# Attention, experts and a tanh-shrink layer in one program: a redrawn opening plan (first scores, small softmax steps, first loads)

## The chip, the core and the metric

The kernel is one program on one core of a Trainium2 chip. The metric is the device time of one execution in microseconds (us), the lower the better; a kernel's time is the median of three executions. Inputs and outputs lie in the core's HBM.

## What is computed

Three layers follow each other, all in float32. The first is local attention: 2 batches, 8 heads, 576 positions, head size 64. Four heads see the last 32 positions ("plain"), four see every fourth of the last 128 ("dilated").

```python
scores = np.where(masks, scale * q @ k.T, -1e9)
attn = np.exp(scores - scores.max(-1)); attn /= attn.sum(-1) + 1e-9
x = (attn @ v)                      # then heads side by side: 1152 x 512
p = domain_probs / (domain_probs.sum(-1) + 1e-9)
x = sum(p[:, e] * (np.maximum(x @ w1[e], 0) @ w2[e]) for e in range(4))   # 512 -> 1024 -> 512
h = x @ w_in;  g = h - np.tanh(h);  out = g @ w_out                       # 512 -> 2048 -> 512
```

## The kernel before, in words

Tokens are handled in two sets, 512 and 640. Each hidden layer is cut into slices of 512 features; a slice needs two loads of `w1` (512 KB each, tile `raw`), two of `w2`, and each weight is split into a high part (a copy) and a low part (a subtraction), tiles `w`. A product is then three matmuls: high by high, high by low, low by high. The activations `x` and hidden values `h` are split in the same way. From the third slice on, the first product is done by a seven-product scheme.

The program isn't written in the order in which it runs. Every operation is first recorded with a duration (`Engine.cost`), its tiles and what it depends on; then the class `Order` lays the operations out in time, engine by engine, several times, and for the first part of the program tries 1,200 random shifts of the due times. What it settles on is emitted, and each engine then runs its own list strictly in that order. So one cost changed in the table can move instructions on every engine. Because one helper records all operations, nearly all rows of the trace carry one line (L331; L729 for loads); tiles tell them apart.

The part that matters here is `first_attention`, for the 512 tokens of the first set. The work is cut into two halves by position, each of plain and dilated heads, so eight softmax "keys", numbered 0 to 7: keys 0 to 3 belong to the first half (0, 1 plain; 2, 3 dilated), 4 to 7 to the second. For a half:

- `open` writes the mask into a PSUM bank with a matmul (tile `p`, 128x384); `scores` adds q by k onto it (64x96 matmuls, `bank<-x,x`);
- `softmax` takes the maximum on VectorE, and then goes one of two ways, by `STYLE`. Style 1: subtract the maximum (VectorE), one exponential over 128x384 (ScalarE), one sum (VectorE). Style 0: four exponentials of 128x96 on ScalarE, each with its own bias and sum (`accum_out`), and two steps on 128x4 that scale the maximum and add 1e-9;
- a multiplication on GpSimd by one over the sum, then `transposes` on TensorE (`bank<-ident,att`), a copy by ScalarE (`w<-bank` 96x512), and `values` (`bank<-w,h` 64x64, where `h` holds v);
- the result is copied to a high part (ScalarE), a low part (VectorE) and a whole.

After four `values` of the first half the first expert's product can begin (`bank<-x,w` 128x256): this document calls its first row the start of the stream. Matmuls of a zero tile (`warm`, tile `zero`) may be put in where TensorE would wait; eleven stand at the start (`WARM`), and more are offered at places in the list, where the planner leaves out those that don't fit.

Loads are all issued by SyncE, in the planner's order. A load that follows eight others waits for the landing of the one eight places before it.

Of the kernel before, what the change touches and what calls it, by code (L numbers as in the profile page):

```python
# [16 lines left out]
ACTF = mybir.ActivationFunctionType  # L17
# [202 lines left out]
class Program:  # L220
# [7 lines left out]
    def __init__(self):  # L228
        self.ops = []
        self.open = None  # L230
        self.fill = False
        self.seek = self.until = 0
        self.hold = None

    def op(self, engine, us, emit, outs=(), ins=(), port=False, data=0.0):
        if self.open is not None:
            assert engine == "tensor"
            self.open[0] += us
            self.open[1].append(emit)
            self.open[2].extend(outs)  # L240
            self.open[3].extend(ins)
            return
        o = Op()
        o.n, o.engine, o.us, o.emit, o.port, o.data = len(self.ops), engine, us, emit, port, data
        o.before, o.after, o.tiles = set(), [], []
        o.fill, o.gone = self.fill, False
        if self.hold is not None and engine not in ("tensor", "sync"):
            o.before.add(self.hold)
        o.tail = self.TAIL[engine]
        regions = {}  # L250
        for views, writes in ((ins, False), (outs, True)):
            for v in views:
                t, region = v if isinstance(v, tuple) else (v.tile, v.region())
                regions.setdefault((id(t), writes), (t, set()))[1].add(region)
        for (_, writes), (t, found) in regions.items():
            if t not in o.tiles:
                o.tiles.append(t)
            for host in t.hosts:
                if host not in o.tiles:
                    o.tiles.append(host)  # L260
            if o.fill == "idle" and t.ring.psum:
                if wrote_by := [n for n, wrote, _ in t.log if wrote]:
                    o.before.add(wrote_by[-1])
                continue
            found = _joined(found)
            for region in found:
                for other, wrote, region2 in t.log:
                    if (writes or wrote) and other != o.n and _meet(region, region2):
                        o.before.add(other)
            if writes:  # L270

                t.log = [
                    x for x in t.log
                    if not any(_covers(region, x[2]) for region in found) or x[0] == o.n
                ]
            t.log.extend((o.n, writes, region) for region in found)
        for t in o.tiles:
            t.touch.append(o.n)
        self.ops.append(o)
# [35 lines left out]
class Engine:  # L315
# [22 lines left out]
    def cost(self, method, kw, outs, ins):  # L338
        n = math.prod(outs[0].shape[1:])
        psum = any(v.tile.ring.psum for v in (*outs, *ins))  # L340
        if self.name == "tensor":
            rows = kw["lhsT"].shape[0] if method == "matmul" else 128
            if method != "matmul":
                return 0.155, False
            if kw["lhsT"].dtype == F32:
                return 0.055 if n == 96 else 0.071, False
            if kw["lhsT"].dtype == BF16:
                return n / 2400.0 + 0.047, False
            return n / 2400.0 + 0.0136, False
        if self.name == "scalar":  # L350
            if "accum_out" in kw:
                return 0.39, False
            each = 0.00183 if outs[0].real_strides()[-1] > 1 or n < 0 else 0.00083
            return (0.172 if any(v.tile.ring.psum for v in ins) else 0.205) + n * each, False
        if self.name == "vector":
            if method == "tensor_reduce":
                n = math.prod(ins[0].shape[1:])
                return 0.152 + n * 0.00105, False
            big = [v for v in ins if math.prod(v.shape[1:]) > 16]
            if psum:  # L360
                return 0.153 + n * 0.00104 + 0.05 * (len(ins) > 2), False
            if n <= 16:
                return 0.18, len(ins) > 1
            if method in ("tensor_tensor", "scalar_tensor_tensor"):
                return 0.15 + n * 0.00104, len(big) > 1
            return 0.16 + n * 0.00052, True
        if method == "tensor_tensor":
            spread = any(0 in v.real_strides() for v in ins)
            return 0.185 + n * (0.00168 if spread else 0.00217), True
        return 0.1 + n * 0.0025, True  # L370


NAMES = ("tensor", "vector", "scalar", "gpsimd", "sync")
# [289 lines left out]
def tile_local_attention_moe_tanhshrink(  # L663
# [56 lines left out]
    def bank(loose=False):  # L720
        return Tile(bank_r, [128, 512], F32, loose=loose).view()
# [11 lines left out]
    def load(view, src):  # L733
        dma(view, src, 4.0 * math.prod(view.shape))
# [170 lines left out]
    class Kind:  # L905
# [51 lines left out]
        def _v(self, t, j, part, b0, n):  # L957

            f = 4 * D
            o = self.parts[part][4][2] + b0 * f  # L960
            a = v[:, o:o + n * f]
            load(t[:, j * f:(j + n) * f], a)

        def load_v(self, i):
            t = self.v[i] = plain32(h_tile(self.g))
# [107 lines left out]

    far_ = {}

    STYLE, COLD, FAR = ((1, 0, 1, 0), (1, 0, 1, 0)), (0,), 6

    class Pair:

# [134 lines left out]
    class Piece(Pair):  # L1214
# [16 lines left out]

        def scores(self, half, c):
            m = masks[0, True]
            if half == 0:
                self.open((0, c), m if self.h.plain else m[:, :BK], not self.h.plain)
            elif c == 0:
                for a in range(2):
                    self.open((1, a), m[:, BK:2 * BK], True)
            with P.group():
                for part, j, qs, ks in self.h.scores(c):  # L1240
                    if j // 2 != half:
                        continue
                    for a in range(2):
                        n = 2 * (j % 2) + part // BQ
                        if half == 0:
                            to = self.sb[0, c][D * a:D * a + D, n * BK:(n + 1) * BK]
                        else:
                            n = 2 * c + j % 2
                            to = self.sb[1, a][part:part + BQ, n * BK:(n + 1) * BK]
                        pe.matmul(  # L1250
                            out=to, lhsT=qs[D * a:D * a + D, :], rhs=ks[D * a:D * a + D, :],
                            start=False, stop=True, skip_group_check=True,
                        )

        def cold(self, key):
            return key[0] in COLD
# [8 lines left out]
        def softmax(self, key):  # L1265
# [6 lines left out]
            if self.style(key):  # L1272
                d, _, _ = self.by_stack(t[:, 0], nm)
                dve.tensor_tensor(out=d, in0=s, in1=spread, op=ALU.add)
                p = self.with_eps(t)
                act.activation(out=p[:, :, :BK], in_=d, func=ACTF.Exp, scale=SCALE)
                dve.memset(ap=p[:, :, BK:], constant=1e-9)
                dve.tensor_reduce(out=r, in_=p, axis=AX.X, op=ALU.add)
                p = p[:, :, :BK]
            else:  # L1280
                act.activation(out=nm[:, :4], in_=nm[:, :4], func=ACTF.Copy, scale=SCALE)
                for j in range(4):
                    ks = slice(j * BK, (j + 1) * BK)
                    act.activation(
                        out=t[:, 1, ks], in_=self.sb[key][:, ks], func=ACTF.Exp,
                        bias=nm[:, j:j + 1], scale=SCALE, accum_out=sm[:, j:j + 1],
                    )
                p, _, _ = self.by_stack(t[:, 1], sm)
                act.activation(out=r, in_=r, func=ACTF.Identity, bias=eps[:, :1])
            dve.reciprocal(out=r, in_=r)  # L1290
            to, _, spread = self.by_stack(t[:, 0], sm)
            pool.tensor_tensor(out=to, in0=p, in1=spread, op=ALU.mult)
# [446 lines left out]
    def first_attention():  # L1739

        def score(half, i, *cs):
            for c in cs or (0, 1):
                both[i].scores(half, c)
# [16 lines left out]
            P.fill = False  # L1760

        idle = bank()
        warm(idle, WARM)
        score(0, 0, 0)
        soft(0)
        warm(idle, 6)
        score(0, 0, 1)
# [3 lines left out]
        warm(idle, 12)  # L1771
        score(0, 1, 1)
        soft(2, 3)
        turn(0)
        turn(1)
        use(0, 0, 0)
        score(1, 0)
        soft(4)
        turn(2)
        use(0, 0, 1)  # L1780
        soft(5)
        turn(3)
        use(0, 1, 0)
        score(1, 1)
        use(0, 1, 1)
        fill(*[("h", 0, 0, f) for f in range(NF)])
        soft(6)
# [42 lines left out]
    da.load_q_half(0)  # L1830
    da.load_k_half(0)
    pa.load_v(0)
    w_load(0, 0)
    da.load_v(0)
    w_load(0, 1)
    pa.load_piece(0, 1)
    pa.load_piece(1, 1)
# [17 lines left out]
    db.load_v_short()  # L1855
    first_exp = spare[1, True][:, :32]
    act.activation(out=first_exp, in_=zero, func=ACTF.Exp)
    P.op("gpsimd", 0.8, lambda: make_identity(nc, ident.real()), [ident], [], True)
    dve.tensor_copy(out=ident_bf, in_=ident)
    emit_consts()  # L1860
    emit_masks(0)
# [84 lines left out]
```

## Time and profile before

| what | value |
|---|---|
| median of three executions | 624.08 us (622.91 to 625.18) |
| profiled execution, its own time | 623.72 us |
| its span, first to last instruction | 621.7 us |
| TensorE busy | 616.5 us, 99% |
| TensorE weight loads busy | 542.8 us, 87% |
| VectorE, ScalarE, GpSimd busy | 379.5, 307.8, 316.1 us |
| mean granted clock of TensorE | 0.999 |

Times in rows are us from the start of the span. A row of the timeline holds a start, the time to the end of the last of its instructions, the engine, the operation with its tiles and its shape, and how many there were; idle time before it and what ended it stand in brackets. A float32 matmul shows as two records, so x16 there are 8 matmuls of the program. TensorE's busy time is nearly the whole span, but matmuls of the zero tile count in it as work.

### The profile page before, as it was taken

Reading aid. Unit: us, or ns where it says so; the run is one execution under the profiler, and the core shown is the slowest. Engines: PE = TensorE matmul, PEld = TensorE weight load, DVE = VectorE, ACT = ScalarE, POOL = GpSimd, SP = SyncE. Lnnn points to the kernel's source line nnn. Section 1 sums busy time; section 2 is a strip of 40 time slices with the busy share of each in tenths; the row PEclk is TensorE's granted clock in tenths of the full one; section 3 lists DMA queues with packets and bytes.
Section 4 is the critical chain, followed back from the end, with each engine's and each line's share of the span. In section 5 each row is a group of like instructions: output and inputs, shape, how many; then the busy total and the mean of one; then the engine's idle time right before and its main releaser. Section 6 shows DMA issues by size and latency. Waiting matters only on the chain.

```text
span 621.7 us, 10650 instructions
## 1 busy us (share of the span) xinstructions
PE 616.5 (99%) x4034; PEld 542.8 (87%) x4034; DVE 379.5 (61%) x718; ACT 307.8 (50%) x744; POOL 316.1 (51%) x284
## 2 busy tenths in 40 slices
PE   9999999999999999999999999999999999999997
PEld 5887798989889889889889889898898988998986
DVE  4856567877776777745424455446877667753652
ACT  6876675654434344424314355343775563551540
POOL 4659982845335435435425459863655563560220
PEclk9999999999999999999999999999999999999999
DMA  8984134164445456322102112330305324110012
GB/s 303 357 289 136 35 103 143 38 214 148 137 135 170 137 155 200 103 69 69 35 34 69 35 35 68 129 119 25 119 1 170 119 84 137 51 53 1 18 51 84
DMA packets 37266, 68.03 MB, mean 109 GB/s; under 512 B 4192, under 2 KB 11488, under 8 KB 37216
## 3 DMA queue, kind: packets, MB, share of 16 engines
q1 hardware_dynamic: 37216, 67.37, 33.2%
q8 instruction: 31, 0.51, 0.3%
q14 instruction: 19, 0.16, 0.1%
HBM read 56.61 MB, written 10.75 MB: 108 GB/s over the span
## 4 chain that ended last, share of the span: by engine, by line
PE 98%; DVE 1%; ACT 0%; issue 0%; DVEq 0%; ACTq 0%
PE bank L331 98%; DVE acc L331 0%; ACT att L331 0%; DVE bank L331 0%; DVE h L331 0%; DVE st L331 0%; DVEq L1942 0%; ACT p L331 0%; DVE att L331 0%; DVE zero L331 0%; DVE eps L331 0%; DVEq L331 0%; ACTq L331 0%
## 5 line engine op out<-in xcount | busy, mean ns | idle before, releaser
L331 PE MATMUL bank<-w,h 128*128 128x512 f32 (+1 forms) x1392 | 323.3, 384 | 0.3
L331 PE MATMUL bank<-x,w 128*128 128x256 f32 (+2 forms) x1992 | 287.3, 298 | 0.0
L331 PEld LDWEIGHTS bank<-x,w 128*128 128x128 f32 x1992 | 277.9, 188 | 9.9
L331 PEld LDWEIGHTS bank<-w,h 128*128 128x128 f32 (+1 forms) x1392 | 240.8, 185 | 50.9 <-DVE acc L331 0.9
L331 POOL TENSOR_TENSOR w<-raw,w 128x512 fp32r<-128x512 f32 x102 | 133.6, 1323 | 144.2 <-ACT w L331 141.2
L331 ACT ACTIVATE h<-bank 128x320 fp32r<-128x320 f32 (+3 forms) x168 | 68.5, 421 | 82.5 <-PE bank L331 65.4
L331 DVE SCALAR_TENSOR_TENSOR acc<-bank,pn,acc 128x512 f32<-128x512 f32 x59 | 44.3, 750 | 76.8 <-PE bank L331 76.6
L331 DVE TENSOR_TENSOR bank<-bank,p 128x320 f32<-128x320 f32 (+1 forms) x132 | 61.0, 466 | 35.2 <-PE bank L331 24.2
L331 ACT ACTIVATE w<-raw 128x512 fp32r<-128x512 f32 x108 | 67.2, 629 | 28.2 <-PE bank L331 21.7
L331 DVE SCALAR_TENSOR_TENSOR att<-att 128x512 int32<-128x512 int32 (+1 forms) x96 | 76.0, 802 | 1.6
L331 DVE SCALAR_TENSOR_TENSOR h<-bank,h 128x320 fp32r<-128x320 f32 (+2 forms) x124 | 55.9, 464 | 26.1 <-ACT h L331 25.1
L331 POOL TENSOR_TENSOR w<-sum,w 128x512 fp32r<-128x512 f32 x36 | 48.7, 1352 | 38.0 <-ACT w L331 37.9
L331 ACT ACTIVATE p<-bank 128x320 f32<-128x320 f32 (+1 forms) x88 | 35.8, 413 | 51.1 <-PE bank L331 50.7
L331 ACT ACTIVATE att<-bank 128x256 f32<-128x256 f32 (+3 forms) x78 | 32.2, 431 | 50.2 <-PE bank L331 42.9
L331 ACT ACTIVATE att<-att 128x512 f32<-128x512 f32 (+2 forms) x40 | 26.2, 655 | 27.7 <-DVE att L331 21.8
L331 DVE TENSOR_TENSOR acc<-bank,acc 128x512 f32<-128x512 f32 (+1 forms) x28 | 18.7, 672 | 33.1 <-PE bank L331 33.1
L331 POOL TENSOR_TENSOR h<-att,h 128x256 fp32r<-128x256 f32 (+1 forms) x28 | 21.8, 800 | 27.0 <-ACT h L331 26.2
L331 POOL TENSOR_TENSOR sum<-raw 128x512 f32<-128x512 f32 x12 | 15.6, 1300 | 34.8 <-DMA raw<-in 14.0
L331 ACT ACTIVATE w<-sum 128x512 fp32r<-128x512 f32 x36 | 22.6, 628 | 20.7 <-PE bank L331 18.9
L331 POOL TENSOR_TENSOR att<-att,st 128x480 f32<-128x480 f32 (+1 forms) x20 | 18.4, 927 | 10.5 <-DVE st L331 9.7
L331 DVE TENSOR_SCALAR att<-att 128x512 int32<-128x512 int32 x32 | 17.2, 538 | 8.9 <-DMA in<-att 7.0
L331 DVE TENSOR_TENSOR bank<-bank,att 128x256 f32<-128x256 f32 (+1 forms) x32 | 14.7, 462 | 9.4 <-ACT att L331 9.1
(72 smaller groups left out, 356.4 us busy)
## 6 DMA issues: line engine op xcount, KB each, us to landing
raw<-in_moe_w_dram SPq DMA_DIRECT2D x40, 512.0 KB, 4.0
att<-in_moe_w_in_dram SPq DMA_DIRECT2D x16, 512.0 KB, 4.6
att<-in_moe_w_out_dram SPq DMA_DIRECT2D x16, 512.0 KB, 4.9
in<-att SPq DMA_DIRECT2D x16, 256.0 KB, 4.0
out<-att SPq DMA_DIRECT2D x16, 256.0 KB, 3.9
raw<-in SPq DMA_DIRECT2D x8, 512.0 KB, 3.7
raw<-out SPq DMA_DIRECT2D x8, 512.0 KB, 3.6
h<-in_v_dram SPq DMA_DIRECT2D x7, 512.0 KB, 6.3
```

The source lines that it names most:

```text
L331: getattr(self.engine, method)(**real)
```

## The change

Seven edits:

- costs: zero-tile matmuls at the start are planned 1.65 times longer, the first half's scores 2 times; `accum_out` on PSUM 0.335 us instead of 0.39; VectorE's memset 0.07; GpSimd's memset and other steps shorter; the identity 0.52 instead of 0.8;
- `STYLE` of the first four keys goes from (1, 0, 1, 0) to (0, 0, 0, 0);
- the two 128x4 steps of style 0 go from ScalarE to VectorE;
- the mask openings of the first half are recorded by a function of their own, after the first scores;
- the second half's scores are recorded earlier, and as work that may fill a wait;
- the dilated v of the first half is recorded ahead of the first weights;
- every load of v takes 96 partitions instead of 128 (`[:BK]`).

```diff
+        if engine == "tensor":
+            us *= self.rate
...
-                return 0.39, False
+                return 0.335 if any(v.tile.ring.psum for v in ins) else 0.39, False
...
-            a = v[:, o:o + n * f]
-            load(t[:, j * f:(j + n) * f], a)
+            load(t[:BK, j * f:(j + n) * f], v[:BK, o:o + n * f])
...
-    STYLE, COLD, FAR = ((1, 0, 1, 0), (1, 0, 1, 0)), (0,), 6
+    STYLE, COLD, FAR = ((0, 0, 0, 0), (1, 0, 1, 0)), (0,), 6
...
-                act.activation(out=nm[:, :4], in_=nm[:, :4], func=ACTF.Copy, scale=SCALE)
+                dve.tensor_scalar(
+                    out=nm[:, :4], in0=nm[:, :4], scalar1=SCALE, scalar2=0.0, op0=ALU.mult, op1=ALU.add,
+                )
...
-                act.activation(out=r, in_=r, func=ACTF.Identity, bias=eps[:, :1])
+                dve.tensor_scalar(
+                    out=r, in0=r, scalar1=1e-9, scalar2=0.0, op0=ALU.add, op1=ALU.add,
+                )
...
+        P.rate = 1.65
         warm(idle, WARM)
+        P.rate = 1.0
+        both[0].begin(0)
         score(0, 0, 0)
+        both[0].begin(1)
+        both[1].begin(0)
+        both[1].begin(1)
         soft(0)
...
+        P.fill = True
+        score(1, 0)
+        score(1, 1)
+        P.fill = False
         turn(0)
         turn(1)
...
     pa.load_v(0)
+    da.load_v(0)
     w_load(0, 0)
-    da.load_v(0)
```

What the planner makes of it is seen in the lists of instructions. On TensorE, at the very start, the kernel before has eleven zero-tile matmuls and then, for each of the four groups of the first half, an opening and its scores (`p` is the mask, `bank` a PSUM bank, `x` q and k); these are the rows of the first three groups and what follows the fourth:

```order
L331 MATMUL bank_135<-x0_78,x0_72 64x96 x8
L331 MATMUL bank_158<-p_84 128x384
L331 MATMUL bank_158<-x0_82,x0_72 64x96 x8
L331 MATMUL bank_181<-p_84 128x384
L331 MATMUL bank_181<-x0_102,x0_96 64x96 x8
L331 MATMUL bank_204<-p_84 128x384
L331 MATMUL bank_204<-x0_102,x0_96 64x96 x8
L331 MATMUL bank_222<-zero_80 32x512
```

At the same place the changed kernel, after eight zero-tile matmuls, has:

```order
L334 MATMUL bank_130<-x0_80,x0_72 64x96 x8
L334 MATMUL bank_159<-p_82 128x384
L334 MATMUL bank_166<-p_82 128x384
L334 MATMUL bank_170<-p_82 128x384
L334 MATMUL bank_159<-x0_87,x0_72 64x96 x8
L334 MATMUL bank_166<-x0_107,x0_98 64x96 x8
L334 MATMUL bank_170<-x0_107,x0_98 64x96 x8
L334 MATMUL bank_230<-p_82 128x384
L334 MATMUL bank_236<-p_82 128x384
L334 MATMUL bank_243<-p_82 128x384
```

The three other openings now stand together behind the first scores, and behind the fourth group come the second half's openings and its plain scores in place of seven zero-tile matmuls. From there to the start of the stream the changed list holds one zero-tile matmul, where the kernel before has eleven.

On SyncE, behind the first six loads, which are the same, the kernel before issues (`h` from `in_v` is v, `raw` is a weight load, `x` is q or k):

```order
L729 DMA h0_109<-in_v_dram 128x1024
L729 DMA x0_72<-in_q_dram 128x256
L729 DMA x0_78<-in_k_dram 128x256
L729 DMA x0_72<-in_q_dram 128x256
L729 DMA x0_82<-in_k_dram 128x256
L729 DMA h0_147<-in_v_dram 128x1024
L729 DMA raw_156<-in_moe_w1_dram 128x2x512
L729 DMA raw_176<-in_moe_w1_dram 128x2x512
L729 DMA x0_183<-in_k_dram 128x768
L729 DMA x0_96<-in_q_dram 128x512
```

and the changed kernel:

```order
L734 DMA x0_72<-in_q_dram 128x256
L734 DMA x0_80<-in_k_dram 128x256
L734 DMA x0_72<-in_q_dram 128x256
L734 DMA x0_87<-in_k_dram 128x256
L734 DMA x0_147<-in_k_dram 128x768
L734 DMA x0_98<-in_q_dram 128x512
L734 DMA h0_161<-in_v_dram 96x1024
L734 DMA raw_172<-in_moe_w1_dram 128x2x512
L734 DMA raw_185<-in_moe_w1_dram 128x2x512
L734 DMA h0_190<-in_v_dram 96x1024
```

All q and k of the second half now go first, then the plain v, the two `w1` loads, and the dilated v last.

On VectorE, about when the weights land, the kernel before takes the first weight copy (`CAST w1`) between softmax steps (`st`, `att`) and low parts of x:

```order
L331 CAST w1_312<-raw_156 128x512
L331 TENSOR_REDUCE st_334<-bank_297 128x4
L331 RECIPROCAL st_291<-st_291 128x4
L331 TENSOR_TENSOR x0_352<-bank_281,x0_337 128x256
L331 TENSOR_REDUCE st_360<-bank_299 128x4
L331 TENSOR_TENSOR att_276<-bank_297,st_334 128x384
L331 CAST w1_378<-raw_176 128x512
```

and the changed kernel takes two copies in a row, from both loads:

```order
L334 TENSOR_REDUCE st_330<-bank_236 128x4
L334 TENSOR_REDUCE st_345<-bank_243 128x4
L334 CAST w1_356<-raw_172 128x512
L334 CAST w1_370<-raw_185 128x512
L334 TENSOR_SCALAR st_330<-st_330 128x4
L334 TENSOR_TENSOR att_382<-bank_243,st_345 128x384
L334 TENSOR_TENSOR x0_397<-bank_358,x0_354 128x256
```

The scaling of key 5's maximum (`st_330`) and the low parts of x now stand behind the copy from the second load.

About 30 us into the program the lists of all engines become the same again, in the same order to the end.

## Rows read from the trace of the kernel before

**Rows 1.** Waits of TensorE from 17 us to the end: total us, times, longest.

```profile
PE bank L331 <- DVE h L331: 0.3, 1, 0.3
```

**Rows 2.** Timeline of TensorE: start us, us, instruction, count.

```profile
1.01 4.88 PE L331 MATMUL bank<-zero 128*32 128x512 bf16 x11 [1.01 <-DVE zero L331]
5.81 0.39 PE L331 MATMUL bank<-p 128*128 128x384 bf16 x1
6.13 0.88 PE L331 MATMUL bank<-x,x 64*64 64x96 f32 x16
...
10.17 1.68 PE L331 MATMUL bank<-zero 128*32 128x512 bf16 x7
11.78 0.64 PE L331 MATMUL bank<-ident,att 128*96 128x128 f32 x4
12.36 0.39 PE L331 MATMUL bank<-zero 128*32 128x512 bf16 x1
...
13.24 0.69 PE L331 MATMUL bank<-w,h 96*64 96x64 f32 x16
13.86 0.50 PE L331 MATMUL bank<-p 128*128 128x384 bf16 x2
14.29 0.89 PE L331 MATMUL bank<-x,x 64*64 64x96 f32 x32
...
16.30 0.82 PE L331 MATMUL bank<-zero 128*32 128x512 bf16 x3
...
20.11 4.52 PE L331 MATMUL bank<-x,w 128*128 128x256 f32 x36
...
48.45 2.95 PE L331 MATMUL bank<-x,w 128*128 128x512 f32 x12
```

**Rows 3.** Timeline of VectorE, same columns.

```profile
7.06 0.56 DVE L331 TENSOR_REDUCE st<-bank 128x4 f32<-128x384 f32 x1 [3.46 <-PE bank L331]
...
10.27 0.18 DVE L331 RECIPROCAL st<-st 128x4 f32<-128x4 f32 x1
...
13.69 0.43 DVE L331 CAST w<-raw 128x512 fp32r<-128x512 f32 x1 [1.07 <-DMA raw<-in_moe_w_dram]
...
15.95 0.42 DVE L331 TENSOR_TENSOR x<-bank,x 128x256 fp32r<-128x256 f32 x1
```

**Rows 4.** Timeline of ScalarE, same columns.

```profile
8.96 0.34 ACT L331 ACTIVATE att<-bank,st 128x96 f32<-128x96 f32 x1
...
9.29 0.33 ACT L331 ACTIVATE att<-bank,st 128x96 f32<-128x96 f32 x1
...
10.39 0.30 ACT L331 ACTIVATE st<-st,eps 128x4 f32<-128x4 f32 x1
...
12.46 0.59 ACT L331 ACTIVATE w<-bank 96x512 f32<-96x512 f32 x1 [0.71 <-PE bank L331]
```

**Rows 5.** Timeline of GpSimd, same columns.

```profile
10.60 1.61 POOL L331 TENSOR_TENSOR att<-att,st 128x384 f32<-128x384 f32 x2 [5.57 <-DVE st L331]
...
14.20 1.27 POOL L331 TENSOR_TENSOR w<-raw,w 128x512 fp32r<-128x512 f32 x1 [0.99 <-DVE w L331]
...
42.68 1.30 POOL L331 TENSOR_TENSOR w<-raw,w 128x512 fp32r<-128x512 f32 x1 [2.09 <-ACT w L331]
```

**Rows 6.** Tile view, both `w1` loads: issue starts (first to last), then us to landing.

```profile
L729 SPq DMA_DIRECT2D raw<-in_moe_w_dram x2: 382/407/432, 6.5 to 7.3; - x2
...
DMA to landing us min/median/max: 7.1/7.4/7.7
```

**Rows 7.** The same view, both first v loads.

```profile
L729 SPq DMA_DIRECT2D h<-in_v_dram x2: 430/431/432, 3.5 to 6.1; - x2
...
DMA to landing us min/median/max: 5.8/6.0/6.3
```

**Rows 8.** The same view, dilated k of the first half.

```profile
L729 SPq DMA_DIRECT2D x<-in_k_dram x1: 442/442/442, 3.1 to 3.1; - x1
...
DMA to landing us min/median/max: 4.2/4.2/4.2
```

More of the change, by code (lines that the diff above doesn't have):

```diff
@@ L231, in __init__ @@
         self.fill = False
+        self.rate = 1.0
         self.seek = self.until = 0
@@ L358, in cost @@
                 return 0.152 + n * 0.00105, False
+            if method == "memset":
+                return 0.07, False
             big = [v for v in ins if math.prod(v.shape[1:]) > 16]
@@ L369, in cost @@
             return 0.185 + n * (0.00168 if spread else 0.00217), True
-        return 0.1 + n * 0.0025, True
+        return (0.15 + n * 0.00085 if method == "memset" else 0.15 + n * 0.0019), True
 NAMES = ("tensor", "vector", "scalar", "gpsimd", "sync")
@@ L1233, in scores @@
             m = masks[0, True]
-            if half == 0:
-                self.open((0, c), m if self.h.plain else m[:, :BK], not self.h.plain)
-            elif c == 0:
+            if half and c == 0:
                 for a in range(2):
                     self.open((1, a), m[:, BK:2 * BK], True)
+            P.rate = 1.0 if half else 2.0
             with P.group():
@@ L1253, in scores, with begin @@
                         )
+            P.rate = 1.0
+        def begin(self, c):
+            m = masks[0, True]
+            self.open((0, c), m if self.h.plain else m[:, :BK], not self.h.plain)
         def cold(self, key):
@@ L1762, in first_attention @@
         idle = bank()
+        P.rate = 1.65
         warm(idle, WARM)
+        P.rate = 1.0
+        both[0].begin(0)
         score(0, 0, 0)
+        both[0].begin(1)
+        both[1].begin(0)
+        both[1].begin(1)
         soft(0)
@@ L1776, in first_attention @@
         use(0, 0, 0)
-        score(1, 0)
         soft(4)
@@ L1783, in first_attention @@
         use(0, 1, 0)
-        score(1, 1)
         use(0, 1, 1)
@@ L1857, in tile_local_attention_moe_tanhshrink @@
     act.activation(out=first_exp, in_=zero, func=ACTF.Exp)
-    P.op("gpsimd", 0.8, lambda: make_identity(nc, ident.real()), [ident], [], True)
+    P.op("gpsimd", 0.52, lambda: make_identity(nc, ident.real()), [ident], [], True)
     dve.tensor_copy(out=ident_bf, in_=ident)
```

## The prediction

> **What bounds the kernel now.** I read TensorE's waits first: from 17 us to the end it waits 0.3 us in all [rows 1]. From there on the time is the sum of TensorE's own rows, and nothing that the other engines do there is on the path, unless it gets late. So the change can only act before, and what it gains must show as an earlier arrival at a row that both kernels have.
>
> Then I read TensorE's timeline ahead of that point [rows 2]. The reader should see there three kinds of rows: real ones, waits, and matmuls of the zero tile, which do no work but count as busy. There are 11 at the start (4.88 us, 0.44 each), 7 at 10.17, 1 at 12.36 and 3 at 16.30 (0.24 each, 1.68/7). Their two prices are also the clock's two levels: 512 columns in 0.44 us is 1.2 GHz, in 0.24 about 2.4. So the higher level was granted somewhere between the end of the eleven and 10.17. The stream of the first expert starts at 20.11.
>
> Last I read what those zero matmuls stood in for: VectorE, ScalarE, GpSimd [rows 3 to 5] and the landings of the loads [rows 6 to 8].
>
> **The change, step by step.** The lists say that 22 zero matmuls become 9: three of 0.44 and ten of 0.24 go, 1.3 + 2.4 = 3.7 us. That is the ceiling of the gain; where the data isn't there, a wait takes their place. I walk the new lists from the start to the stream, with durations of the rows.
>
> *First scores.* Eight zero matmuls end 3 x 0.44 earlier, so the first opening begins at 5.81 - 1.3 = 4.5. Opening 0.32 (5.81 to 6.13), scores 0.88: done at 5.7. The three openings that were moved behind it: two take 0.43 (13.86 to 14.29), so 0.65 for three, 6.35. They delay the second group and save nothing by themselves, but they fill what would be a wait for loads: the dilated k lands at 3.1 + 4.2 = 7.3 [rows 8], and the two dilated groups follow the plain one at 7.25. Three groups, 2.65: done at 9.0, against 10.17 before.
>
> What these groups cost at the lower clock isn't in a row, since I can't tell at which level the 0.88 ran. Bounds: 0.88 and twice that. I take one group as slow, the one that now runs ahead of the time at which the kernel before had ended its eleven; this puts 0.4 to 0.9 on the first group.
>
> *Softmax of the first half.* All four keys are now of style 0: maximum 0.56 on VectorE [rows 3], scaling, then 16 exponentials at 0.33 from start to start (8.96 to 9.29) [rows 4], 5.3 us on ScalarE, in a row. The small steps aren't in the trace on VectorE; nearest is the reciprocal of the same 128x4, 0.18 [rows 3], bounds 0.1 and the 0.30 that adding 1e-9 takes on ScalarE [rows 4]. Twelve of them are 2.2 us of VectorE, which is hidden behind the exponentials; one stands on the path. First exponential at 5.7 + 0.56 + 0.18 + 0.2 for handing over = 6.65, with the slow first group 7.1, last one done at 12.4 (12.0 to 12.9). Moving the steps takes 0.3 per key out of ScalarE's chain; style 0 for two more keys puts some 0.7 back for each (4 x 0.33 for one pass of 0.5 to 0.6). GpSimd's multiplications (0.80 each [rows 5]) keep up.
>
> *First values.* Two copies of 0.59 [rows 4] end at 13.0 and 13.6. The plain v is now behind all q and k, 1,536 KB after the first six loads; before, the same 1,536 KB stood up to the end of the second v, which landed at 6.1 + 6.3 = 12.4 [rows 7]. So it lands at 12.4 instead of 9.3: later, but in time. Values 13.1 to 13.7 (0.62, 13.24 to 13.86 [rows 2]), transposes 0.58 (11.78 to 12.36), values 14.9, transposes 15.5. The second half's plain and dilated scores (0.89 a group of 16) lie in the waits ahead, 9.0 to 13.1, where the ten zero matmuls were.
>
> *The two waits that now decide.* Both `w1` loads have the same number of bytes ahead of them in both kernels, so they land at 13.6 and 15.0 as before [rows 6]. (a) VectorE's second copy of weights waits for 15.0, and behind it, in order, stands the scaling for key 5, for this the first exponential of key 5 on ScalarE, behind this the copy of key 3's transposes, behind this the last values: 15.0 + 0.43 + 0.18 + 0.1 = 15.7; + 0.34 = 16.05; + 0.59 = 16.65; + 0.62 = 17.3. (b) The dilated v is behind these loads: 384 KB at 1.4 us per 512 KB (13.6 to 15.0) is 1.05, so 16.05; values 16.7, one zero matmul 0.24, values 17.6. The softmax, (a) and (b) end within 0.3 us of each other. The stream starts at 17.3 to 17.6; I take 17.45, against 20.11: 2.65 earlier. The loads' queue doesn't run dry: a load waits for the eighth before it, and for these that is landed by 8, five us ahead.
>
> *Behind the start.* VectorE does 0.56 and two low parts of 0.42 after 15.7, so x is split by 17.1. GpSimd makes the low parts of the weights, 1.27 each [rows 5]: the first two at 15.9 and 17.2, then two multiplications, then the third at 21.1 and the fourth at 22.4. The stream (0.126 a row, 4.52/36) has 24 rows and two transposes ahead of the third: 17.45 + 3.0 + 1.15 + 0.25 = 21.85, and wants the fourth at 23.4. So 0.75 and 1.0 us are to spare. Later the first weight of the second slice is ready at 42.68 + 1.30 = 44.0 and used at 48.45: 4.5 us to spare, more than 2.65, and the loads ahead of it are shorter by a quarter of each v. From about 30 us on the lists are the same, and 0.3 us of waits [rows 1] can't swallow the gain.
>
> **The sum.** The profiled execution took 623.72, span 621.7. 623.72 - 2.65 = 621.1. It stands 0.36 under the median, 624.08; from the median, 621.4.
>
> **The rivals.** 0.3% is what a measurement of this kernel can tell from no change: 1.87 us, 622.2.
>
> *The clock is granted late (the other side).* TensorE's real work between 4.5 and 17.45 is 4 x 0.88 + 2 x 0.89 + 8 openings (1.9) + 4 x 0.58 + 4 x 0.62 + 0.24 = 12.2 us, so only 0.7 us is to spare. At the lower level it takes up to twice as long, so a grant at T costs (T - 4.5)/2 - 0.7. The gain is used up at T = 11.2: from there on the kernel is slower than before. Granted at 14, it costs 4.05, 625.5. For it: eight dense matmuls instead of eleven, then sparse ones. Against it: before, the clock survives the sparse rows from 12.4 to 16.3, and at 10.17 it is up after some 4 us of just such scores. [...]
>
> *A v of 96 partitions is no faster.* No row has a load of 96 partitions. If each takes the 1.4 us of 128, the weights land 0.35 later, the dilated v 0.7 later, at 16.75; values 17.4, zero matmul, values 18.25: the stream is 0.65 later, 622.0. [...] I price by bytes, since the loads overlap with others, but keep this as an end.
>
> *The stream starves.* VectorE's copies for the third and fourth weight stand behind low parts that need the last values. If ScalarE gives these 1.5 us later than I count, the spare 0.75 is gone, and as much again is lost at the second half's transposes: 622.7.
>
> *The plan changes nothing.* The zero matmuls stood in real waits, and loads that land at the same time keep the waits: 623.7 to 624.4. Against it: before, TensorE runs without a wait of its own from 17 us on [rows 1], with the last zero matmuls at 16.30, so loads don't set 20.11; its order does.
>
> *More than forecast.* If all scores run at the higher clock and the copies come in time, 620.4.
>
> **How the numbers follow.** Forecast (621 to 622) 0.50; more 0.08; v no faster 0.12; starved 0.12; no change 0.10; clock 0.08. Faster than 622.2: 0.50 + 0.08 + 0.07 of the v case = 0.65. Within: the rest of v, starved, no change, 0.27. Slower: 0.08. The range from 620.1 to 623.6 leaves out the clock and most of no change, 0.17.
>
> **What would show it.** First opening near 4.5; four groups done near 9; sixteen exponentials in a row on ScalarE from about 7 to 12.4; `w1` landing at 13.6 and 15.0, plain v at 12.4, dilated v at 16.05; a copy on VectorE that waits for the second load; the stream at 17.45; TensorE without waits behind it. I am wrong if scores take twice 0.88, if the stream starts after 18.5, or if it starts early and waits for GpSimd's weights.

## The result: slower, and the profile after

The changed kernel takes 629.79 us (median of 7 executions, 627.58 to 631.19), the kernel before 624.25 beside it: ratio 1.0080, 95% interval 1.0055 to 1.0106. 621.4 was forecast, with a range of 620.1 to 623.6: the measured time lies above all of it. The profiled execution took 628.54, span 626.5 (621.7 before), mean granted clock 0.991 (0.999). Three executions of the versions tried below took 749.76, 1216.32 and 1546.92 us; they are left aside as slow.

TensorE's timeline of the changed kernel answers to [rows 2]:

```profile
0.94 3.33 PE L334 MATMUL bank<-zero 128*32 128x512 bf16 x8 [0.94 <-DVE eps L334]
4.21 0.34 PE L334 MATMUL bank<-p 128*128 128x384 bf16 x1
4.47 0.88 PE L334 MATMUL bank<-x,x 64*64 64x96 f32 x16
...
9.07 0.66 PE L334 MATMUL bank<-p 128*128 128x384 bf16 x3
...
12.99 0.69 PE L334 MATMUL bank<-w,h 96*64 96x64 f32 x16
...
17.43 1.07 PE L334 MATMUL bank<-w,h 96*64 96x64 f32 x16 [2.00 <-DMA h<-in_v_dram]
18.44 0.61 PE L334 MATMUL bank<-zero 128*32 128x512 bf16 x1
18.98 1.12 PE L334 MATMUL bank<-w,h 96*64 96x64 f32 x16
20.03 2.93 PE L334 MATMUL bank<-x,w 128*128 128x256 f32 x12
...
45.04 0.86 PE L334 MATMUL bank<-w,h 128*128 128x512 f32 x3
48.33 6.73 PE L334 MATMUL bank<-w,h 128*128 128x512 f32 x21 [2.42 <-ACT h L334]
54.89 2.93 PE L334 MATMUL bank<-x,w 128*128 128x512 f32 x12
```

Down to 15 us nearly all is as forecast (TensorE waits 0.85 for a load of k ahead of 7.60). Then come two waits, for the dilated v (2.00) and for ScalarE (2.42), and behind each the rows get longer: 12 rows of the stream take 2.93, where 36 took 4.52 before. The windows of both kernels (start, end and length; busy us of PE, PEld, DVE, ACT, POOL with counts; granted clock as a share of the full one; busy share of the DMA engines; GB/s) show two more things. After:

```profile
14.00:20.00 6.00, 4.00 (x56) 2.89 (x53) 3.20 (x13) 2.96 (x12) 4.06 (x5) 0.79 1.04 259
20.00:26.00 6.00, 6.00 (x36) 5.94 (x35) 3.44 (x9) 3.61 (x10) 4.07 (x4) 0.64 1.05 286
26.00:46.00 20.00, 19.78 (x211) 16.98 (x210) 8.95 (x24) 12.09 (x37) 7.90 (x10) 1.00 1.06 266
```

and before:

```profile
14.00:20.00 6.00, 6.00 (x127) 4.11 (x125) 4.35 (x12) 5.45 (x23) 4.37 (x4) 1.00 1.05 407
20.00:26.00 6.00, 6.00 (x57) 5.93 (x53) 4.65 (x13) 5.32 (x21) 4.33 (x6) 1.00 1.07 341
26.00:46.00 20.00, 20.00 (x206) 17.28 (x206) 12.09 (x27) 15.91 (x46) 11.65 (x12) 1.00 0.93 309
```

The granted clock falls to half (17.5 to 24.4, and again 48.2 to 51.7), and the DMA engines, no less busy (1.04 against 1.05), move 259 GB/s instead of 407. That is the larger finding: the same bytes take longer, though those of v are fewer. In the packed traces a packet of 4 KB, one row of v, took 159 ns between 10 and 26 us in the kernel before and 269 in the changed kernel (medians), one of 4,608 bytes, from a load of q with 128 partitions, 182 and 274 (medians), one of 2 KB, as the weight loads have them, 87 and 112 (means). Of those of 2 KB in the changed kernel, the ones from 10 to 12 us, among 55 packets of v, took 136 ns, the ones from 12 to 14, among 7, 88 (medians).

Of the clock's two levels the traces show this: in the kernel before, the zero matmuls of 512 columns start 427 ns apart ahead of 5.3 us and 216 ns apart from 10.17 to 11.5, 1.2 and 2.4 columns per ns. The 1.2 and 2.4 GHz of the prediction and the expectations stand for these two rates; the frequency itself is in no trace.

Where the time went, at rows that both have: the stream starts level (20.03, 20.11). Half the clock until 24.4 costs 2.2 from there on: the 24 rows of w,h begin at 45.04 instead of 42.85.

```profile
42.85 5.76 PE L331 MATMUL bank<-w,h 128*128 128x512 f32 x24
```

The wait for ScalarE and two short ones behind it, 3.1, and half the clock again bring the second slice's first product to 54.89 instead of 48.45 [rows 2], 6.4 late. Of that 1.3 come back in equal rows between 113 and 609 us, where the changed kernel is steadily a little quicker; 0.4 came back before. 4.8 are left, the difference of the spans.

### The profile page after: what moved, and what is told of

Same layout as the page of the kernel before. It is cut to its first block, busy times and chain, and to the rows that moved or that the text cites. A ratio compares the mean times of both kernels' runs of the same rounds, so it can differ in the third digit from the quotient of the medians.

```text
span 626.5 us, 10644 instructions
## 1 busy us (share of the span) xinstructions
PE 615.9 (98%) x4021; PEld 544.6 (87%) x4021; DVE 381.2 (61%) x724; ACT 307.5 (49%) x750; POOL 316.9 (51%) x284
## 4 chain that ended last, share of the span: by engine, by line
PE 95%; DMA 3%; DVE 1%; SPq 0%; ACT 0%; issue 0%; POOL 0%; DVEq 0%
PE bank L334 95%; DMA h<-in_v_dram 1%; DMA raw<-in_moe_w_dram 1%; DMA x<-in_k_dram 1%; SPq L734 0%; DVE acc L334 0%; ACT x L334 0%; ACT h L334 0%; ACT w L334 0%; POOL x L334 0%; DVE x L334 0%; DVEq L1962 0%; ACT acc L334 0%; DVE psum_r L334 0%
## 5 line engine op out<-in xcount | busy, mean ns | idle before, releaser
L334 DVE TENSOR_TENSOR bank<-bank,p 128x320 f32<-128x320 f32 (+1 forms) x132 | 60.9, 466 | 35.6 <-PE bank L334 20.9
L334 DVE SCALAR_TENSOR_TENSOR att<-att 128x512 int32<-128x512 int32 (+1 forms) x96 | 79.5, 838 | 1.6
L334 ACT ACTIVATE w<-sum 128x512 fp32r<-128x512 f32 x36 | 22.6, 627 | 20.9 <-PE bank L334 18.9
```

The source lines that it names most:

```text
L334: getattr(self.engine, method)(**real)
```

## Experiments

Each kernel was timed beside the kernel before on the same chip (medians 623.35 to 624.48 us), and its ratio is to that.

**Narrow loads.** In the changed kernel, v again with 128 partitions (its planned size left alone, so that every list stays):

```diff
-            load(t[:BK, j * f:(j + n) * f], v[:BK, o:o + n * f])
+            dma(t[:, j * f:(j + n) * f], v[:, o:o + n * f], 4.0 * BK * n * f)
```

> The changed kernel with one edit undone: its five long loads of v write 128 partitions again (512 KB instead of 384); the planner is given the old size, so every engine's list is the same. Theory A (loads of 96 partitions slow all transfers that are in flight with them): 4 KB packets take about 159 ns again instead of some 270, the second w1 load lands near 15.5 instead of 16.0, the dilated v near 17 or before, the second slice's first weights near 42 instead of 47.35; no wait of 2 us for v and none of 2.4 us near 45; the clock stays up; 621 to 623 us. Theory B (the order of the loads and the sparse list of TensorE are to blame, the clock falls in the wait): the waits and the fall of the clock stay, 628 to 630 us.

In the kernel before, the reverse, alone (lists again the same), and then with 112 partitions:

```diff
-            a = v[:, o:o + n * f]
-            load(t[:, j * f:(j + n) * f], a)
+            a = v[:BK, o:o + n * f]
+            dma(t[:BK, j * f:(j + n) * f], a, 4.0 * 128 * n * f)
```

> The kernel before with loads of v of 96 partitions alone, its lists unchanged. Theory A: packets in flight with a v take 1.5 times as long or more, the second slice's first weights land some 4 to 5 us later than 41.95, TensorE waits for them near 46, 627 to 630 us. Theory B: nothing but 25% fewer bytes of v, the weights land up to 2.9 us earlier, 623.5 to 625 us.

> The kernel before with v loads of 112 partitions, lists unchanged: does the slowness go with the bytes, with 96, or with not being 128? [...] Theory B: 159 ns, 623.5 to 625 us.

And with 96 only for the four v loads of the first set:

```diff
+            m = BK if self.g == 0 else 128
-            a = v[:, o:o + n * f]
-            load(t[:, j * f:(j + n) * f], a)
+            a = v[:m, o:o + n * f]
+            dma(t[:m, j * f:(j + n) * f], a, 4.0 * 128 * n * f)
```

> The kernel before, with only the four v loads of the first set taking 96 partitions (all issued by 12.4 us); the later ones take 128. Lists as before. Theory of narrow loads, local: what is in flight beside a narrow load is slow, and the rate recovers behind the last of them: 240 to 350 GB/s from 10 to 26 us, about 300 to 310 from 26 to 46, the second slice's first weights land at 44 to 45 (41.95 before, 46.63 with all v loads narrow), time 625 to 627. Rival, only the later and wider v loads of the second set matter, or the sum of all bytes: landing within 0.7 of 41.95 and 624 to 624.6.

Measured: the change without narrow loads 623.93, ratio 0.9988 (0.9975 to 1.0001); the kernel before with them 628.58, 1.0075 (1.0050 to 1.0099); with 112 partitions 631.41 in its one run, far above the 623.5 to 625 of Theory B; with four narrow loads 626.98, 1.0044 (1.0024 to 1.0064). Windows of the changed kernel with 128, then of the kernel before with 96, then with four narrow loads:

```profile
14.00:20.00 6.00, 4.33 (x58) 3.42 (x58) 3.81 (x14) 3.50 (x13) 4.13 (x4) 0.80 1.04 405
20.00:26.00 6.00, 6.00 (x49) 6.00 (x49) 3.36 (x11) 5.01 (x18) 4.69 (x5) 0.92 1.09 345
```

```profile
14.00:20.00 6.00, 5.57 (x111) 3.59 (x109) 4.17 (x12) 5.22 (x21) 4.08 (x4) 1.00 1.05 338
20.00:26.00 6.00, 6.00 (x79) 5.81 (x71) 4.93 (x12) 5.06 (x22) 3.77 (x5) 1.00 1.07 267
26.00:46.00 20.00, 18.32 (x192) 15.57 (x191) 10.87 (x24) 12.73 (x34) 9.34 (x10) 0.91 0.97 258
```

```profile
20.00:26.00 6.00, 6.00 (x52) 6.00 (x53) 4.36 (x12) 5.31 (x20) 4.31 (x6) 1.00 1.07 277
26.00:46.00 20.00, 18.58 (x197) 15.41 (x195) 11.51 (x25) 11.75 (x32) 8.36 (x9) 1.00 1.00 312
```

One edit of the seven makes the slowdown, in either kernel, and it acts on what is in flight beside such a load too (the packets of 2 KB, and of 4,608 bytes, above): behind the last of four narrow loads the rate is back at 312. These four cost about 3 of the 4 us, as the local reading wants; the second slice's weights landed at 46.2 in that profile, later than I expected. In that one run 112 partitions are no better than 96 (288 GB/s from 10 to 26 us, 297 with 96, 375 with 128). In the changed kernel with 128 the loads land as expected (second `w1` at 15.47, dilated v at 16.76, the second slice's first weight at 42.16), but a wait of 1.67 and a fall of the clock stay, which I had not expected:

```profile
16.90 0.69 PE L334 MATMUL bank<-w,h 96*64 96x64 f32 x16 [1.67 <-ACT att L334]
...
19.10 2.51 PE L334 MATMUL bank<-x,w 128*128 128x256 f32 x12
```

The stream starts at 19.10, 1.0 earlier than before, but at half the clock until 20.9, and at 32.5 us the lead is gone. That profiled execution, 622.41, is the fastest of the twelve. The seven with a mean clock of 0.999 or more took 622.81 to 624.01, the other five 622.41 to 624.96; what the eleven others kept of the lead is not shown.

Why loads of 96 partitions are slower than loads of 128, and slow others too, no run here shows; the cause stays open.

**The clock.** Zero matmuls kept in the place of the wait before the last values, nine in the changed kernel, eight in the one with 128 partitions; and in the kernel before the eleven in the middle left out:

```diff
-            if not o.gone:
+            if not o.gone or o.n in self.program.keep:
...
+                n0 = len(P.ops)
...
+                if not h.plain and c == 0:
+                    P.keep.update(range(n0, n0 + 9))
```

```diff
-            if not o.gone:
+            if not o.gone and not (o.fill == "idle" and o.start > 7.0):
```

> The changed kernel with nine more matmuls of the zero tile ahead of the dilated values, in TensorE's wait of 2.0 us at 15.4. Theory B (the fall of the clock is what costs): the clock stays at 2.4 GHz behind 17.4, the stream gains 3 us and the whole 3 us, 626 to 627 us. Theory A (the loads decide): the stream runs 3 us ahead and then waits that much longer for the second slice's weights, which land at 47.3 as before; the whole gains at most 1 us, 628.5 to 630 us.

> The changed kernel with v of 128 partitions, and eight more matmuls of the zero tile in the wait that is left there (14.96 to 16.90), lists otherwise as in the changed kernel. Theory C (what is left of the loss is the clock, which falls after this wait, from 17.54 to 20.95): the clock stays at 2.4 GHz, values and stream rows behind 17 us take their usual time, TensorE reaches the first w rows that it now has at 32.52 some 1.5 us earlier, 622 to 622.8 us. Theory D (the stream is held by weights and copies that come late, not by the clock): the clock stays, but TensorE waits instead, 32.5 as before, 623.5 to 624.5 us.

> The kernel before without its eleven zero-tile matmuls behind 10 us (seven, one, three), all else unchanged: waits of 1.6, 0.3 and 0.75 us are left in their places. Theory C in its strong form (an idle TensorE of more than a microsecond among sparse rows lets the clock fall): it falls once near 12 to 16, half speed for 3.4 us or more costs 1 to 2 us, 625.3 to 626.5 us. Rival: what stands around the waits keeps the clock up, the matmuls only filled waits, 624 to 624.6 us.

Measured: 631.07, ratio 1.0096 (1.0064 to 1.0128); 623.40, 0.9993 (0.9977 to 1.0009); 623.51, 0.9986 (0.9972 to 0.9999). With eight the clock stays at 1.00 from 14 to 26 us (0.80 and 0.92 without), and the stream starts at 19.20 with its 12 rows in 1.69. Yet the time can't be told from that of the kernel before. The profiled execution waits 3.54 us at 43 us:

```profile
46.71 0.97 PE L335 MATMUL bank<-w,h 128*128 128x512 f32 x3 [3.54 <-ACT h L335]
```

But at 627.65 it is the slowest of the eleven, and the second slice's first weight landed at 45.74 in it (42.16 in the profile without the zero matmuls). The eight with a mean clock of 0.999 or more took 622.65 to 623.50, the three at 0.997 624.92 to 627.65. So whether the eight keep part of the gain, and what takes the rest, is not shown. In the changed kernel with nine, the loads are still late in the profiled execution, the slowest of four (a wait of 1.73 up to 20.8), and the clock falls all the same. Without its fillers the kernel before waits 1.23 us and less, its clock stays (0.999), and nothing is lost: the zero matmuls only stood in waits. So in the changed kernel the clock is a second loss, behind a longer wait, not the first.

**Two queues.** First, in the kernel with 128 partitions, the dilated v is loaded ahead of the weights, and the scaling for key 5 stands ahead of VectorE's weight copies (`P.ahead[a] = b` emits operation a just before b; `P.cast` is the first weight copy):

```diff
+                if key == (1, 1) and self.h.plain:
+                    P.scaled = len(P.ops) - 1
...
+    P.ahead[len(P.ops) - 1] = len(P.ops)
...
+    P.ahead[P.scaled] = P.cast
```

> The changed kernel with v of 128 partitions, and two instructions moved in the lists: the dilated v is loaded ahead of both w1 loads, and VectorE scales key 5's maximum ahead of its two weight copies. The two waits of the prediction, (a) and (b), are gone. Theory C: TensorE doesn't wait 1.7 us at 15, the clock stays, the stream starts near 17.2 (weights 1.3 us later set it), 621 to 622.3 us, faster than with fills. Theory D: the weights that land 1.3 us later (15.5 and 16.8) hold the stream or its third and fourth weight, no gain against the 128 partitions alone, 623.5 to 624.5 us.

Measured: 624.07, ratio 0.9991 (0.9981 to 1.0001). In the profiled execution the stream starts at 19.18, 0.9 earlier than before, the clock is whole (as in three of the ten executions), and the gain is gone in a wait of 1.65 for ScalarE that starts at 43.3. The changed kernel's ScalarE says why:

```profile
47.37 0.63 ACT L334 ACTIVATE w<-raw 128x512 fp32r<-128x512 f32 x1 [6.29 <-DMA raw<-in_moe_w_dram]
47.91 0.37 ACT L334 ACTIVATE h<-bank 128x256 fp32r<-128x256 f32 x1
...
48.77 0.63 ACT L334 ACTIVATE w<-raw 128x512 fp32r<-128x512 f32 x1 [0.19 <-DMA raw<-in_moe_w_dram]
49.30 0.37 ACT L334 ACTIVATE h<-bank 128x256 fp32r<-128x256 f32 x1
```

In the kernel before, at the same place:

```profile
41.97 0.63 ACT L331 ACTIVATE w<-raw 128x512 fp32r<-128x512 f32 x1 [1.22 <-DMA raw<-in_moe_w_dram]
42.51 0.37 ACT L331 ACTIVATE h<-bank 128x256 fp32r<-128x256 f32 x1
```

ScalarE stands for 6.29 us at the copy of a weight that TensorE wants only at 54.89. Behind it in its list stands a hidden value that TensorE wants at 45.9: its row there ends the wait of 2.42 <-ACT h. In the kernel before, too, a hidden value stands behind that copy; it does no harm, since the load lands just in time. So I put the four weight copies (and their low parts) behind the hidden values, in the changed kernel, in the version with the dilated v ahead, and in the kernel before:

```diff
+        last = max(self.program.relus, key=lambda n: self.ops[n].start)
+        for i, n in enumerate(self.program.weights):
+            key[n] = (self.ops[last].start, last + 0.1 + 0.01 * i)
...
+        if n == 1:
+            P.weights += [len(P.ops), len(P.ops) + 1]
...
+        if n == 0 and half == 1:
+            P.relus.append(len(P.ops))
```

> The changed kernel, with one block moved on ScalarE: the four copies of the second slice's first weights stand behind the three copies of hidden values (h from a bank, 128x256) that they stood ahead of and between. Theory of the queue: in the changed kernel TensorE's wait of 2.42 us at 45.5 (and 0.36 and 0.31 behind it) is not for the weights but for the hidden values queued on ScalarE behind a copy that waits for the load at 47.35. Moved, TensorE runs through, the clock doesn't fall at 48.24, and the time is 4.0 to 4.8 us less, 625.0 to 625.8; the first wait (2.0 us ahead of the stream) and the clock's fall behind it stay. Rival, the weights are late themselves: the second slice's first product, wanted at about 51.4, waits for low parts of weights that GpSimd makes from 48 on, 1.3 us each, and the gain is under 1 us, 628.8 to 629.8.

> The plan of the change with v loads of 128 partitions and the dilated v ahead of the weights (624.07 so far), with the same block moved on ScalarE: hidden values ahead of the copies of the second slice's weights. Theory of the queue: the gain that this plan makes at the start of the stream (about 0.9 us) ends in a wait of 1.65 + 0.44 us at 42.9, which is ScalarE's, behind the load at 43.98; moved, the wait goes and the time is 1.5 to 2.5 us less, 621.6 to 622.6, below both kernels. Rival, the loads decide: they come at the same time and the wait only moves to the second slice's first product, 623.6 to 624.4.

> The kernel before, with the same block moved on ScalarE. In its profiled execution the load lands at 41.95, just as the copy is wanted, and TensorE waits for nothing. Theory of the queue: nothing to gain where the load lands in time, a few tenths where it lands later (43.3 in another execution of the same lists), so 623.6 to 624.2. Rival: the moved block delays the second set's softmax on GpSimd or ScalarE, which nothing in the kernel before hides, and the time is over 624.6.

Measured: 627.38, ratio 1.0053 (1.0035 to 1.0071); 623.34, 0.9978 (0.9961 to 0.9996); 623.97, 0.9998 (0.9984 to 1.0012). ScalarE and TensorE of the first:

```profile
45.80 0.38 ACT L335 ACTIVATE h<-bank 128x256 fp32r<-128x256 f32 x1 [1.05 <-PE bank L335]
47.38 0.64 ACT L335 ACTIVATE w<-raw 128x512 fp32r<-128x512 f32 x1 [1.19 <-DMA raw<-in_moe_w_dram]
```

```profile
21.13 2.93 PE L335 MATMUL bank<-x,w 128*128 128x256 f32 x12
...
45.60 5.75 PE L335 MATMUL bank<-w,h 128*128 128x512 f32 x24
51.19 2.93 PE L335 MATMUL bank<-x,w 128*128 128x512 f32 x12
```

The load lands no earlier (47.38), and TensorE no longer waits for it: from the stream's start to 51.19 it takes 30.1 us instead of 34.9. I had expected 4.0 to 4.8 us less. By the medians 2.4 came, by the ratios 1.7 (1.0080 and 1.0053, whose intervals overlap). In the profile the dilated v landed 1.1 later here, and of the lead at 51 us 1.3 is lost later, 1.24 of it in a wait for VectorE that ends at 92.46. The rival (weights themselves late) is refuted by the product at 51.19, which waits for nothing. In the kernel before nothing changes, as expected. The second gains 0.2%, less than expected; in its profile TensorE waits 2.44 us at 16.4, <-DVE att, and then has half the clock:

```profile
18.79 0.38 PE L336 MATMUL bank<-zero 128*32 128x512 bf16 x1 [2.44 <-DVE att L336]
```

```profile
17.57 0.70 DVE L336 CAST w<-raw 128x512 fp32r<-128x512 f32 x1 [0.93 <-DMA raw<-in_moe_w_dram]
18.19 0.54 DVE L336 TENSOR_TENSOR att<-bank,st 128x384 f32<-128x384 f32 x1
```

Its two executions with a mean clock of 0.999 or more took 621.22 and 621.71, the other nine, 0.994 to 0.997, took 623.07 to 625.24.

That wait is the same kind of queue, on VectorE: the subtraction that empties a bank for the next matmul stands behind two weight copies that wait for loads. So the last version takes it ahead of both, and the second copy behind the low parts of x:

```diff
+                if key == (1, 0) and not self.h.plain:
+                    P.taken = len(P.ops)
...
+            if h.plain and half == 0 and c == 0:
+                P.low = len(P.ops)
...
+        if n == 0 and name == "a12":
+            P.cast2 = len(P.ops)
...
-    P.ahead[P.scaled] = P.cast
+    P.ahead[P.scaled] = P.ahead[P.taken] = P.cast
+    P.behind[P.cast2] = P.low
```

> The version of the experiment before (v loads of 128 partitions, dilated v ahead of the weights, hidden values ahead of the second slice's weight copies; 623.34) with two more rows moved on VectorE: the subtraction that empties the bank which the zero matmul and the last values take over stands ahead of both weight copies, not behind them, and the second weight copy stands behind the low parts of x. Theory of the queue: TensorE's wait of 2.44 us at 16.35 (<-DVE att) is for that bank, since the subtraction stands behind copies that wait for loads at 16.2 and 17.6; moved, the last values run at 16.4, the stream starts at 17.1 to 18.0 without a fall of the clock, and the time is 1.3 to 2.9 us less, 620.4 to 622.0. Rival, the loads decide: the stream waits for the low part of the second weight (load at 17.6, copy, 1.27 on GpSimd) or the second slice for its own, and the time is 622.8 to 624.0.

Measured: 621.16 (9 executions, 620.57 to 621.95), ratio 0.9958 (0.9943 to 0.9972), faster than both kernels, all nine at a mean clock of 0.999 or 1.0. VectorE and TensorE of this version:

```profile
14.54 0.56 DVE L336 TENSOR_TENSOR att<-bank,st 128x384 f32<-128x384 f32 x1
15.28 0.43 DVE L336 CAST w<-raw 128x512 fp32r<-128x512 f32 x1 [0.18 <-DMA raw<-in_moe_w_dram]
15.62 0.75 DVE L336 TENSOR_TENSOR x<-bank,x 128x256 fp32r<-128x256 f32 x2
17.59 0.43 DVE L336 CAST w<-raw 128x512 fp32r<-128x512 f32 x1 [1.22 <-DMA raw<-in_moe_w_dram]
```

```profile
16.49 0.45 PE L336 MATMUL bank<-w,h 96*64 96x64 f32 x8
17.93 0.45 PE L336 MATMUL bank<-w,h 96*64 96x64 f32 x8 [0.98 <-issue]
18.31 1.70 PE L336 MATMUL bank<-x,w 128*128 128x256 f32 x12
...
47.66 2.94 PE L336 MATMUL bank<-x,w 128*128 128x512 f32 x12
```

The copy still waits 1.22 us for its load, but nothing that TensorE needs stands behind it. The last values begin at 16.49, the stream starts at 18.31, 1.8 earlier than in the kernel before. Of this 0.8 is left at 47.66 (0.5 goes in a wait for GpSimd at 20.5, the rest in short gaps); the other 1.8 us of its span (619.1) come later, 1.4 of them in the equal rows behind 107 us. A wait of 0.98 stands in the middle of the last values; its cause, which the trace calls issue, I did not follow up.

## Why the prediction was wrong, step by step

- **First scores, softmax, first values: right.** First opening 4.21 (4.5), scores at 0.88 with no slow group, four groups done 9.07 (9.0), sixteen exponentials from 6.25 to 12.0 (7 to 12.4), small steps 0.14 to 0.17 on VectorE (0.18; but 0.65 and 0.77 for two that ran beside a multiplication on GpSimd), first values 12.99 (13.1). The bound of 0.4 to 0.9 for the low clock wasn't needed.
- **The two waits: the order right, the price wrong.** The step that failed is "384 KB at 1.4 us per 512 KB is 1.05". It takes a rate from loads of 128 partitions and gives it to loads of 96, and the sentence ahead of it, that the weights "land at 13.6 and 15.0 as before", goes by bytes too and fell with it. By the tile view the plain v landed at 12.57 (12.4) and the first `w1` at 13.92 (13.6), but the second at 16.00 (15.0) and the dilated v at 17.30 (16.05), and the loads behind them fell further back, to 47.35 for the second slice's first weight (41.95 before). "The loads ahead of it are shorter by a quarter of each v" had the wrong sign. The rival of a v no faster named the loads that are to blame, but gave each narrow load the time of 128 partitions and no more, 0.65 us in all; the two comparisons of the narrow load alone give 4.1 and 5.9 us (medians: 628.58 against 624.48; 629.79 against 623.93).
- **The clock: not in the sum.** I priced a late grant, not a second fall. It was granted by the first scores (at 3.9 us by the packed trace; at 6.0 in the kernel before); it fell behind a wait of 2.0 us between sparse rows. My own walk left TensorE a wait of 0.55 there (15.5 to 16.05); the late loads made it 2.0. Of the 2.6 us by which the stream starts after 17.45, 1.4 is the late v (its values begin at 17.43 instead of 16.05), and 1.1 the half clock in the two groups of values and the zero matmul (2.60 instead of 1.48). Behind the stream's start it cost the 2.2 counted above.
- **Behind the start: the spare was read from the wrong row.** "Used at 48.45: 4.5 us to spare" asks who uses the weight. The question was what stands behind its copy on ScalarE: a hidden value wanted at 43. The spare was next to nothing (ScalarE waits until 41.97, and TensorE goes on without a wait), and with 128 partitions too it ends the gain in the profiled executions that wait for ScalarE there (3.54 and 1.65). The lists are also not the same from 30 us on: on ScalarE one hidden value that stood ahead of the first weight copy's wait now stands behind it, and weight copies stand between the others.
- **"The plan changes nothing"** describes the change without its narrow loads best (623.93), but not for the reason it gave: in the profiled executions the start does gain 0.9 to 1.0 us, and a half clock or ScalarE's queue takes it back. So the narrow loads alone don't account for the missing 2.65. The last version keeps the new plan and gains 2.2 us; in its profile 1.8 of the 2.65 are there at the stream's start, 1.2 are left at 107 us, and the other 1.4 come from the equal rows, which no term of the sum held. That its 621.16 lies near the 621.4 forecast is luck.
- **A slip.** The starving rival adds up to 622.9 (621.4 and twice 0.75), not 622.7; no conclusion hangs on it.

## What to carry to other kernels

Don't price a load by its bytes when its shape is one that the trace has not shown: run it alone first, and look at the rate of all loads beside it. For a row that waits for a load, the spare time is not that of its own reader but of the first row behind it on the same engine (here a hidden value, wanted at 45.9, behind ScalarE's wait of 6.29 us for a weight wanted at 54.89); put copies of late weights behind what another engine needs now. A plan that packs real work more tightly also takes away the slack that hid such rows, so look at the next two waits before booking the gain.

## What the runs showed of the hardware that I had not expected

- Beside loads of 96 partitions the other transfers go slower too: 259, 286 and 266 GB/s in windows that had 407, 341 and 309, with the DMA engines as busy (1.04, 1.05 and 1.06 against 1.05, 1.07 and 0.93). Packets of 4,608 bytes, from a load of 128 partitions, took 274 ns there instead of 182.
- In the profiled executions the granted clock fell to half in or behind waits of 2.0 us (changed kernel), 1.67 (the same with 128 partitions), 2.44 and 2.83 between sparse rows, and of 2.42 and 3.54 for ScalarE; it stayed whole after waits of 1.50 and 1.65 in one execution. These are single executions, and no limit follows from them.
- Equal rows behind 107 us take 1.2 to 1.4 us less in the profile of every kernel drawn by the new plan, whatever its loads (the row at 604.04 of the kernel before stands at 608.79 in the changed one, where it had been 6.07 late at 113.62). There the matmuls of 128x512 start 232.2 ns apart on average in the changed kernel, 233.0 in the kernel before; why is open.
